# Packed attention and a token-mixing MLP on one core: two heads by 64 partitions, 128-token query tiles, 64x32 PV tiles, single PSUM banks, and one computed issue order

## The chip, the cores and the metric

The kernel runs on one core of one Trainium2 chip. The metric is the device time of one execution in microseconds (us). "The kernel before" took 183.92 us (median of three runs, 183.14 to 187.25). Some executions of one kernel take longer at a lower granted clock; a run over 1.5% above the fastest of its kernel is called slow, and the ratios below use the other, fast runs alone, with a 95% interval.

Engines are named as in the profile: PE is the TensorE matmul, PEld its weight load, DVE the VectorE, ACT the ScalarE, POOL the GpSimd, SP the SyncE. A "q" after a name (SPq) is the engine's instruction queue, for example while it issues a DMA.

## The reference

Eight batches, eight heads, 576 tokens, head width 64, and 32 "pack" queries per head:

```python
def sm_attn(qq, kk, vv):                     # softmax attention, scale 1/8
    s = scale * np.matmul(qq, kk.transpose(0, 1, 3, 2))
    a = softmax(s)
    return np.matmul(a, vv)
p_packed = sm_attn(p, k, v)                  # 32 packed rows per head
x = sm_attn(q, p_packed, p_packed)           # back to 576 tokens
# x as [batch, 576, 512]
W_tok = (x @ w_q) @ (x @ w_k).T / 8          # [576, 576] per batch
out = np.maximum(W_tok @ x, 0) @ w_out       # [batch, 576, 512], float32
```

Neither kernel forms the 576 x 576 matrix: both compute `y` (64 x 512, from `w_k`, the second softmax and the packed rows), then `mix = y^T wq^T`, a relu, and the output product.

## The kernel before

A row of 576 tokens is cut so that each partition holds 18 of them: 32 partitions per head, four heads side by side, two groups of four heads. Three streams run against each other: `stage_a` of batch i+1 (first attention, to the packed rows), `stage_c` of batch i (second attention, to `y`), and `stage_e` of batch i-1 (mix and output). Each is a generator cut into steps, and `together` interleaves the steps in proportion.

```python
    NG, NP = 2, 4
    R, QP = 18, 32
    # PSUM pools: tp (2 banks), sc (2), acc (2 tiles), w (2)
    def rows(x, b):
        return x[b].rearrange("(G pos) (sh sl) d -> (pos sh) G sl d", G=NG, sl=R)

    def load_cast(x, b, name):                       # k and q: cast by the GpSimd's DMA
        t = inpool.tile([P, NG, R, Dh], bf16, tag=name, name=name)
        nc.gpsimd.dma_start(t, rows(x, b))
    def load_v(b):                                   # v: loaded as fp32, cast by POOL
        nc.sync.dma_start(t, rows(v, b))
    # ... first loads, in this order: k0, p0 (POOL's queue), v0 (SP's), q0, weights, p, k1, v1, q1

        def pvm(c):                                  # 144 matmuls per batch, 32x32 tiles
            for r in range(3):
                for par in range(2):
                    s = 2 * (3 * c + r) + par
                    for G in range(NG):
                        for pos in range(NP):
                            m = slice(pos * QP, (pos + 1) * QP)
                            nc.tensor.matmul(
                                pv[m, G, 0:Dh + 1], e1[m, r, G, par, :], v_sb[m, G, s, 0:Dh + 1], ...)

    def stage_e(b, st):
        for j in range(NJ):                          # mix: 64 rows of contraction
            nc.tensor.matmul(ps, y[:, j * P:(j + 1) * P], wqT[:, 0:512], start=True, stop=True)
            nc.scalar.activation(relu[:, j, 0:512], ps, RELU)
            yield
        # ...
        for ci, (c0, sz) in enumerate(chunks):       # five chunks, the last of 64 tokens
            for j in range(NJ):
                nc.tensor.matmul(ps[0:sz], relu[:, j, c0:c0 + sz], wout_w[:, j, :], ...)
                if j == 1:
                    yield
            # ... copy to o
            for i in range(sz // QP):                # 18 output DMAs of 64 KB per batch
                nc.sync.dma_start(o_v[c, x, r], o[i * QP:(i + 1) * QP])
            yield

    def together(*streams):
        todo = []
        for order, (steps, gen) in enumerate(streams):
            todo += [((i + 0.5) / steps, order, gen) for i in range(steps)]
        for _, _, gen in sorted(todo, key=lambda x: x[:2]):
            next(gen, None)
```

The softmax here doesn't subtract the row's maximum and nothing guards it: scores larger than these inputs give would overflow.

## Time and profile before

| | before |
|---|---|
| median of runs | 183.92 us |
| span of the profiled run (its time 187.25 us) | 185.8 us |
| PE busy, whole span | 139.5 us (75%) |
| first score transposes / first query score | 14.5 / 31.0 us |
| one batch in the steady state | 17.6 us |
| last `y` copy to the end | 16.0 us |

The profiled run is the longest of the three. Its clock explains that: see the PEclk row below.

The first fence is from the page of the kernel before: the span, the busy time of each engine (share of the span, number of instructions), the clock granted to PE in 40 slices (tenths of full speed), and the chain of waits that ended last, by engine.

```profile
span 185.8 us, 6608 instructions
...
PE 139.5 (75%) x2854; PEld 89.6 (48%) x2880; DVE 87.2 (47%) x197; ACT 74.8 (40%) x164; POOL 68.4 (37%) x75
...
PEclk9999999975559999999999999999999999999996
...
PE 45%; DVE 18%; DMA 9%; issue 7%; ACT 7%; SPq 5%; POOL 5%; DVEq 0%; POOLq 0%; ACTq 0%
```

The second fence is the windows view of the kernel before. The cuts are at ScalarE's copies of `y`, one per batch. The columns after the window are its length, each engine's busy time and number of instructions, the granted clock, the DMA share and the GB/s.

```profile
core 0: us, PE busy (x) PEld busy (x) DVE busy (x) ACT busy (x) POOL busy (x), PEclk, DMA share, GB/s
45.70:66.60 20.90, 19.51 (x352) 12.72 (x349) 9.73 (x22) 9.00 (x21) 9.05 (x11) 0.74 0.51 101
66.60:154.50 87.90, 79.05 (x1760) 50.23 (x1781) 51.12 (x115) 44.38 (x101) 35.22 (x34) 1.00 0.64 163
154.50:169.80 15.30, 11.71 (x118) 7.04 (x120) 7.86 (x17) 7.36 (x17) 3.14 (x3) 1.00 0.31 79
169.80:185.80 16.00, 6.81 (x30) 2.44 (x28) 3.44 (x5) 3.59 (x7) 0.00 (x0) 0.91 0.38 98
```

The second row holds five batches: 87.90 / 5 = 17.6 us each, PE busy for 79.05 of 87.90 us (90%). The row above it is a batch partly at half clock, and it took 20.9 us.

The third fence is the chain of waits of the kernel before through one steady batch, from one `y` copy to the next (start, duration, what; short pieces left out).

```profile
84.28 0.60 ACT y L336
...
87.54 0.56 DVE qT L242
...
88.56 0.60 DVE rs L257
...
89.65 1.05 POOL a_1955 L261
...
92.16 0.55 PE out_ps L357 x2
...
92.73 0.70 DVE o_sb L365
...
93.45 0.31 SPq L369
...
95.26 1.65 SPq L369
...
97.90 1.64 DMA out_dram<-o_sb
...
99.55 0.70 DVE o_sb L365
...
100.30 0.59 PE out_ps L357 x2
...
101.86 0.60 ACT y L336
```

### The profile page before, as it was taken

How to read it: one execution, taken by the hardware profiler on the slowest of the kernel's cores; microseconds unless marked ns; L12 is line 12 of the kernel's file. 1: busy time of each engine (PE TensorE's matmuls, PEld its weight loads, DVE VectorE, ACT ScalarE, POOL GpSimd, SP SyncE). 2: the span in 40 equal slices, each digit the busy share in tenths (PEclk: the TensorE clock that was granted, in tenths of full speed). 3: DMA queues.
4: the chain of work that ended last, by engine and by line, in shares of the span. 5: the costliest groups of instructions: out<-in, count | busy, mean ns of one | idle time of the engine just before them, and what ended most of it. 6: DMA issues, size and time to landing. Idle time of an engine off the chain costs nothing.

```text
span 185.8 us, 6608 instructions
## 1 busy us (share of the span) xinstructions
PE 139.5 (75%) x2854; PEld 89.6 (48%) x2880; DVE 87.2 (47%) x197; ACT 74.8 (40%) x164; POOL 68.4 (37%) x75
## 2 busy tenths in 40 slices
PE   0008457768999889988998998799979987787820
PEld 0006436654766556645663665376546654443300
DVE  6004024832357348545754673468357633743220
ACT  2002114324453356336633753483347436625400
POOL 7636045335424372445327342704352420420000
PEclk9999999975559999999999999999999999999996
DMA  5999999990941489849964996374450144044153
GB/s 187 335 237 183 256 283 213 280 257 12 179 79 31 120 138 246 299 105 156 282 240 90 207 322 190 93 175 163 109 131 11 40 106 115 4 112 121 49 141 87
DMA packets 17133, 29.66 MB, mean 160 GB/s; under 512 B 5840, under 2 KB 6352, under 8 KB 17104
## 3 DMA queue, kind: packets, MB, share of 16 engines
q0 software_dynamic: 8016, 10.36, 33.4%
q1 hardware_dynamic: 9088, 18.88, 32.9%
q8 instruction: 22, 0.36, 0.8%
q14 instruction: 7, 0.06, 0.1%
HBM read 30.15 MB, written 9.44 MB: 213 GB/s over the span
## 4 chain that ended last, share of the span: by engine, by line
PE 45%; DVE 18%; DMA 9%; issue 7%; ACT 7%; SPq 5%; POOL 5%; DVEq 0%; POOLq 0%; ACTq 0%
PE out_ps L357 11%; DVE o_sb L365 6%; DMA k_sb<-in_k_dram 6%; PE e_ps L248 5%; SPq L369 5%; PE qT_ps L238 5%; PE pv_ps L178 5%; PE kT_ps L152 4%; DMA out_dram<-o_sb 3%; PE mix_ps L344 3%; DVE rs L257 3%; DVE qT L242 3%; PE aT_ps L268 3%; ACT y L336 3%; PE e_ps L165 2%
## 5 line engine op out<-in xcount | busy, mean ns | idle before, releaser
L357 PE MATMUL out_ps<-wout_w,relu 128*128 128x512 bf16 (+1 forms) x134 | 41.1, 382 | 4.4 <-DVE o_sb L365 2.1
L365 DVE COPY o_sb<-out_ps 128x512 f32<-128x512 f32 (+1 forms) x32 | 22.1, 690 | 20.1 <-PE out_ps L357 13.4
L242 DVE COPY qT<-qT_ps 128x768 bf16<-128x768 bf16 x24 | 13.4, 557 | 19.1 <-PE qT_ps L238 19.1
L207 POOL TENSOR_TENSOR ppb<-pp,mask 128x256 bf16<-128x256 bf16 x16 | 10.4, 671 | 32.4 <-DVE pp L202 32.4
L345 ACT ACTIVATE relu<-mix_ps 128x512 bf16<-128x512 f32 x32 | 18.8, 596 | 7.7 <-PE mix_ps L344 7.7
L357 PEld LDWEIGHTS <-relu 128*128 128x128 bf16 (+1 forms) x160 | 12.8, 101 | 10.8 <-issue 8.1
L248 PEld LDWEIGHTS <-qT 128*96 128x96 bf16 x192 | 12.1, 135 | 7.4 <-DVE qT L242 4.8
L152 PE MATMUL kT_ps<-ident,k_sb 128*128 128x128 bf16 x144 | 14.4, 248 | 0.7 <-DVE kT L156 0.7
L156 DVE COPY kT<-kT_ps 128x768 bf16<-128x768 bf16 x24 | 13.3, 552 | 3.3 <-PE kT_ps L152 2.5
L238 PE MATMUL qT_ps<-ident,q_sb 128*128 128x128 bf16 x144 | 13.7, 239 | 1.2 <-ACT pT L127 1.2
L344 PE MATMUL mix_ps<-wqT,y 64*128 64x512 bf16 x32 | 13.2, 412 | 1.2 <-ACT y L336 0.8
L269 DVE COPY aT<-aT_ps 128x384 bf16<-128x384 bf16 x24 | 7.6, 316 | 13.1 <-PE aT_ps L268 13.1
L136 PE MATMUL pT_ps<-ident,p_nat 128*64 128x128 bf16 x32 | 2.1, 312 | 14.1 <-POOL ident masks.py:199 14.1
L238 PEld LDWEIGHTS <-q_sb 128*128 128x128 bf16 x144 | 9.6, 108 | 5.0 <-issue 4.9
L324 ACT ACTIVATE wqT<-wq_ps 64x288 bf16<-64x288 f32 x16 | 6.5, 404 | 13.3 <-PE wq_ps L322 13.3
L152 PEld LDWEIGHTS <-k_sb 128*128 128x128 bf16 x144 | 10.8, 112 | 1.5 <-issue 1.0
L363 ACT ACTIVATE o_sb<-out_ps 128x512 f32<-128x512 f32 x8 | 4.8, 597 | 12.8 <-PE out_ps L357 11.6
L275 PE MATMUL wk_ps<-pqk,aT 128*96 128x64 bf16 x96 | 8.7, 213 | 0.7 <-issue 0.5
L165 PE MATMUL e_ps<-pT,kT 128*32 128x64 bf16 x576 | 9.2, 202 | 0.0
L278 ACT ACTIVATE wk<-wk_ps 96x128 bf16<-96x128 f32 x24 | 6.4, 268 | 5.8 <-PE wk_ps L275 5.7
L136 PEld LDWEIGHTS <-p_nat 128*64 128x64 bf16 x32 | 1.8, 167 | 14.2 <-DMA p_nat<-in_p_dram 12.0
L85 POOL CAST v_bf_86<-v_in 128x2304 bf16<-128x2304 f32 x4 | 8.5, 2116 | 0.0
(292 smaller groups left out, 239.6 us busy)
## 6 DMA issues: line engine op xcount, KB each, us to landing
v_in<-in_v_dram SPq DMA_DIRECT2D x8, 1152.0 KB, 9.9
out_dram<-o_sb SPq DMA_DIRECT2D x144, 64.0 KB, 1.7
k_sb<-in_k_dram POOLq DMA_DIRECT2D x8, 576.0 KB, 8.9
q_sb<-in_q_dram POOLq DMA_DIRECT2D x8, 576.0 KB, 11.4
wout_w<-in_moe_w_out_dram POOLq DMA_DIRECT2D x1, 512.0 KB, 17.2
p_nat<-in_p_dram POOLq DMA_DIRECT2D x1, 224.0 KB, 12.2
wqk<-in_moe_w_q_dram POOLq DMA_DIRECT2D x1, 64.0 KB, 11.7
wqk<-in_moe_w_k_dram POOLq DMA_DIRECT2D x1, 64.0 KB, 11.4
```

The source lines that it names most:

```text
L152: nc.tensor.transpose(ps[:, r, G, :], k_sb[:, G, s:s + 2, :].rearrange("a r d -> a (r d)"), ident)
L156: nc.vector.tensor_copy(kTs[c], ps)
L165: nc.tensor.matmul(ps[m, r, G], kT[:, r, G, m], pT[:, b, G * NP + pos], start=True, stop=True)
L178: nc.tensor.matmul(pv[m, G, 0:Dh + 1], e1[m, r, G, par, :], v_sb[m, G, s, 0:Dh + 1], start=s == 0 and G == 0, stop=s == R - 1, skip_group_ ...
L207: nc.gpsimd.tensor_tensor(ppb[:, G], pp[:, G, 0:1, :].to_broadcast((P, NP, Dh)), mask, op=MULT)
L238: nc.tensor.transpose(ps[:, r, G, :], q_sb[:, G, s:s + 2, :].rearrange("a r d -> a (r d)"), ident)
L242: nc.vector.tensor_copy(qTs[c], ps.rearrange("a r G (pos s) -> a (G pos) r s", s=QP))
L248: nc.tensor.matmul(ps[:, :, h, :], qT[:, h].rearrange("a r s -> a (r s)"), ppT[:, h], start=True, stop=True)
L344: nc.tensor.matmul(ps, y[:, j * P:(j + 1) * P], wqT[:, 0:512], start=True, stop=True)
L345: nc.scalar.activation(relu[:, j, 0:512], ps, RELU)
L357: nc.tensor.matmul(ps[0:sz], relu[:, j, c0:c0 + sz], wout_w[:, j, :], start=j == 0, stop=j == NJ - 1)
L365: nc.vector.tensor_copy(o[0:sz], ps[0:sz])
```

## The change

Its stated intent is another layout and another way of issuing:

- two heads by 64 partitions, nine rows of tokens on each, so a batch fills the partitions with four pairs of heads;
- query tiles of 128 tokens instead of 96; the rests of 64 tokens of two batches share one output tile;
- PV as 72 matmuls on 64x32 tiles into two banks, instead of 144 on 32x32 tiles;
- the mix contracts over 128 rows (half of them zero), and wq and wk come out of one group of matmuls;
- 8 single PSUM banks, named one by one, instead of pools;
- the first k block is loaded first, uncast, in two halves; v is cast by its DMA and no longer by POOL;
- output DMAs of up to 512 KB, 20 in all, instead of 144 of 64 KB;
- all steps of all batches issued from one list, `ORDER`, that was computed beforehand.

The diff, cut to its core:

```diff
+ORDER = """
+LD.v0 LD.q0 LD.W0 LD.W1 PX.0=0 PXb.0 PXa.0 LD.PRA LD.k1 KT.0.0=0 KT.0.1=1 KE.0.0 KE.0.1 LD.v1
+S1.0.0=1 LD.q1 KT.0.2=0 X1.0.0 KT.0.3=2 KE.0.2 KT.0.4=3 KE.0.3 KE.0.4 S1.0.1=2 S1.0.2=3 X1.0.1
 ... (step.batch.part=bank; some 55 lines)
+"""
-    NG, NP = 2, 4
-    R, QP = 18, 32
+    U, R, G = 4, 9, 64
     def rows(x, b):
-        return x[b].rearrange("(G pos) (sh sl) d -> (pos sh) G sl d", G=NG, sl=R)
+        return x[b].rearrange("(u i) (g r) d -> (i g) u (r d)", i=2, r=R)
 ...
+    k0 = rows(k, 0)
+    nc.sync.dma_start(k32[:, 0:2], k0[:, 0:2])
+    nc.sync.dma_start(k32[:, 2:4], k0[:, 2:4])
 ...
+    MCH = ((0, 8), (8, 16), (16, 18))
+    def PV(b, c, bk=None):
+        m0, m1 = MCH[c]
+        for f in range(2 * m0, 2 * m1):
+            u, r = f // R, f % R
+            for i in range(2):
+                rhs = ...                                # 64 columns of v and 64 of ones
+                nc.tensor.matmul(T["pv", b][i][u * L:(u + 1) * L, :],
+                                 T["e1", b][halves(i), f // 2, f % 2, :], rhs,
+                                 start=r == 0, stop=r == R - 1, skip_group_check=True)
 ...
+    def MX(b, j, bk):
+        nc.tensor.matmul(ps, T["y", b][:, j * P:(j + 1) * P], rhs, start=True, stop=True)
 ...
+    def OE(b, t):                                        # two tiles, then one 512 KB DMA
+        copy("AVAV"[t], o[:, t % 2], T["ot", b, t])
+        if done[b, tp] == 2:
+            nc.sync.dma_start(dst.rearrange("g (s m) -> g s m", s=2), ...)
 ...
     with tc.manual_schedule():
-            together(*streams)
+        for item in ORDER.split():
+            name, _, bk = item.partition("=")
+            f = name.split(".")
+            if f[0] == "LD":
+                load(f[1])
+                continue
+            steps[f[0]](*args)
```

In `ORDER`, KT/QT are the key and query transposes, S1/S2 the scores, X1/X2 the exponentials, RS/RR/AM the second softmax (AM on POOL), AT its transpose, WKQ, GM and Y the steps to `y`, MX/RL the mix and relu, OT/OE the output product and copy, LD a load. KE, QE, AE, WE, GE and YE are the copies of these results out of PSUM.

## The prediction

> **What bounds the kernel now.** Three stretches.
> (1) Start: the chain of waits begins with the first k load (issued at 1.2 us, landed 11.8 us), behind 2.3 MB of v; the first score transposes run at 14.5 us, the PE then waits 3.5 us for no visible reason ("issue", 20.9 us, probably instruction fetch), and the first q transposes run only at 29.5 us.
> (2) Steady state: the y copies of ScalarE, one per batch, come at 66.6, 84.3, 101.9, 119.7, 137.1, 154.5 us: 17.6 us per batch. By the windows view PE is busy 90% there, DVE 10.2 us, ACT 8.9, POOL 7 per batch. So PE bounds it. From about 39 to 56 us the granted clock is 0.5 and that batch takes 20.9 us.
> (3) Tail: 16 us from the last y copy to the end. SP issues 144 output DMAs at 0.71 us each (41 in 29.1 us) and is behind at the end.
>
> **PE per batch.** The Trainium skill (TensorE: Matmul & The Clock Gate, "Back-to-back issue gap") gives N/2.4+2.5 ns. The timeline agrees: six transposes of 128 take 0.35 us (58 ns), 20 output matmuls 4.67 us (233 ns). From start-to-start times I sum about 16.0 us per batch before. Estimate after:
> - output matmuls 20 to 18 (the 64-row rests of two batches share a tile): 4.6 to 4.0
> - mix at 128 rows instead of 64: four cost 0.36 each now, 0.22 after: 1.44 to 0.9
> - wk and wq merged: 1.6 to 0.9
> - PV 144 matmuls (10 ns each, four tiles at once) to 72 with N=128, two row tiles at once into two banks: 1.5 to about 1.9, a loss
> - S1 72 of 32 columns to 36 of 64: about equal, 0.9
> - transposes: k same, q 18 to 20, aT 12 to 10 of full width; S2 24 at 128 weight columns: equal or slightly less
> Sum about 14.0 us: 2 us less per batch.
>
> **Other engines per batch, estimated from durations in the trace.** POOL loses the v cast (2.12 us). DVE: 10.2 to about 10.3 (two output copies and g fewer, two relus of about 0.66 more). ACT: 8.9 to about 10.3. DMA: v now cast-loaded, input packets 2304 B instead of 4608; output 20 DMAs of up to 512 KB instead of 144. 4.7 MB per batch at about 350 GB/s is 13.5 us: a second bound near PE.
>
> **Critical path.** Start: k0 is loaded first, uncast and in halves; it should land at 5 to 8 us, and the first q scores run at about 16 us instead of 31: 12 to 14 us gained after the slower fp32 transposes. Steady: 7 x 2 = 14 us. Tail: about 5 us (split relus, SP queue empty). Together 32 us from 184: 152. Counted otherwise: PE saturated from 17 us, 110 us of work at 90%, 6 us of tail: 145.
>
> **Predicted: 148 us, range 139 to 158.** Chances: faster 0.97, within 2% 0.02, slower 0.01.
>
> **What would show it.** y copies 15 to 16 us apart; first q-score matmul before 18 us; PE busy sum near 115 us; 72 PV matmuls in about 1.9 us; no v cast on POOL; SP without lag at the end; last y copy to end 10 to 11 us.
>
> **What would make it wrong.** PV row tiles that don't overlap (then 53 ns each, +2 us per batch, 164 us); 2304-byte packets slow enough that DMA bounds it (PE waiting on k, q, v, 155 to 160); ACT or DVE late in the strict computed order, with PE waiting on bank releases; half clock for long stretches (+3 us each).

## The result, and the profile after

The changed kernel took 137.48 us (median of four runs, 136.22 to 138.82) against 183.72 for the kernel before on the same chip; the ratio of fast runs is 0.749, interval 0.743 to 0.755. Ratios here are the mean time of one kernel's fast runs over that of the other's in the same rounds, so not quite the ratio of the medians quoted. The result is faster than the whole predicted range.

The page of the changed kernel, the same lines:

```profile
span 135.5 us, 4623 instructions
...
PE 114.5 (85%) x1991; PEld 79.8 (59%) x1991; DVE 82.4 (61%) x222; ACT 73.9 (55%) x167; POOL 51.4 (38%) x64
...
PEclk9986998699999999999999999999999999999999
...
PE 66%; ACT 12%; DVE 10%; issue 5%; DMA 2%; ACTq 0%
```

The windows view of the changed kernel; the cut at 30.80 is the first `y` copy, 116.40 and 123.60 the last two, and the second row holds six batches:

```profile
17.00:30.80 13.80, 11.08 (x259) 9.46 (x257) 8.74 (x27) 7.76 (x22) 9.32 (x12) 0.88 1.22 207
30.80:116.40 85.60, 78.14 (x1487) 56.03 (x1485) 57.18 (x142) 52.15 (x119) 30.52 (x35) 1.00 0.84 183
116.40:123.60 7.20, 7.18 (x74) 4.12 (x72) 5.24 (x13) 4.63 (x12) 2.43 (x3) 1.00 0.36 146
123.60:135.50 11.90, 6.45 (x32) 2.41 (x30) 3.18 (x5) 4.37 (x8) 0.00 (x0) 1.00 0.50 199
```

A batch takes 85.60 / 6 = 14.3 us instead of 17.6. PE's busy share in that row is 91%, hardly more than the 90% of before. SPq and the output DMA have nearly left the chain.

Where the 50.3 us between the two profiled spans lie:

| stretch | before | after | difference | predicted |
|---|---|---|---|---|
| start to the first `y` copy | 45.7 | 30.8 | 14.9 | 12 to 14 |
| first to last `y` copy (seven batches) | 124.1 | 92.8 | 31.3 | 14 |
| last `y` copy to the end | 16.0 | 11.9 | 4.1 | 5 |

In the middle stretch PE's busy sum falls from 19.51 + 79.05 + 11.71 = 110.3 to 78.14 + 7.18 = 85.3 us, that is by 25.0, and the rest falls by 6.3 us. The half-clocked batch before was busy 19.51 us against 79.05 / 5 = 15.8 in the five after it, so 3.7 of the 25.0 us are the clock of that run; about 21 us are less busy time in other ways.

PE's busy time per batch in the full-clock windows, worked out from start-to-start times in the two traces (five batches before, six after), beside what the prediction assumed:

| matmuls | before | after | assumed after |
|---|---|---|---|
| output | 4.42 | 3.83 | 4.0 |
| PV | 1.52 | 1.58 | 1.9 |
| mix and its rest | 1.62 | 1.01 | 0.9 (mix alone) |
| k transposes | 1.37 | 1.13 | same as before |
| q transposes | 1.12 | 1.25 | about 10% more |
| second scores | 1.29 | 0.94 | "equal or slightly less" |
| first scores | 0.87 | 0.90 | 0.9 |
| wk and wq | 1.70 | 0.86 | 0.9 |
| aT, g, y and small ones | the rest | the rest | |
| all | 15.8 | 13.0 | 14.0 |
| PE not busy | 1.8 | 1.25 | 1.6 (at 90%) |

In the window of the kernel before, 20 of the 100 output matmuls left no record (there are 100 weight loads and 80 matmuls), so 4.42 is a little low; with the gaps filled in by hand it is about 4.5, an estimate.

So a first theory offers itself. **Theory A:** the mechanism was right (PE bounds the steady state) and only the sum was off: PE's work fell by 2.8 us a batch instead of 2. **Theory B:** PE's work did not set the pace, neither before nor after; the order of the steps did, by keeping PE fed while other engines' links run beside it. Smaller rivals: POOL relieved of the v cast (C), the 128-row mix (D), the earlier start being worth more than its share (E), the merged output DMAs (F).

### The profile page after: what moved, and what is told of

Its sections match the earlier page's. It is cut to its first block, busy times and chain, and to the rows that moved or that the text cites. A ratio compares the mean times of both kernels' runs of the same rounds, so it can differ in the third digit from the quotient of the medians.

```text
span 135.5 us, 4623 instructions
## 1 busy us (share of the span) xinstructions
PE 114.5 (85%) x1991; PEld 79.8 (59%) x1991; DVE 82.4 (61%) x222; ACT 73.9 (55%) x167; POOL 51.4 (38%) x64
## 4 chain that ended last, share of the span: by engine, by line
PE 66%; ACT 12%; DVE 10%; issue 5%; DMA 2%; ACTq 0%
PE out_ps L463 20%; PE pv_ps L274 10%; PE qT_ps L332 6%; PE kT_ps L239 6%; PE aT_ps L381 4%; PE e_ps L256 4%; PE e_ps L350 3%; PE mix_ps L433 3%; ACT relu L437 2%; PE wkq_ps L401 2%; DMA out_dram<-o 2%; DVE kT L123 2%; PE g_ps L413 2%; ACT e L356 2%; PE wkq_ps L397 2%
## 5 line engine op out<-in xcount | busy, mean ns | idle before, releaser
L463 PE MATMUL out_ps<-wout,relu 128*128 128x512 bf16 x128 | 31.0, 379 | 2.1 <-ACT relu L437 1.7
L372 POOL TENSOR_TENSOR a<-e,rr 128x512 bf16<-128x512 f32 (+1 forms) x24 | 21.2, 901 | 29.9 <-DVE rr L367 25.8
L463 PEld LDWEIGHTS <-relu 128*128 128x128 bf16 x128 | 11.6, 98 | 13.9 <-ACT relu L437 2.5
L123 DVE COPY qT<-qT_ps 128x1024 bf16<-128x1024 bf16 (+1 forms) x24 | 13.2, 595 | 6.7 <-PE qT_ps L332 6.6
L274 PE MATMUL pv_ps<-v_sb,e 64*32 64x128 bf16 x576 | 13.7, 221 | 1.3 <-issue 1.3
L362 DVE TENSOR_REDUCE rs<-e 128x16 f32<-128x512 f32 (+1 forms) x24 | 13.3, 576 | 1.3 <-ACT e L356 1.2
L274 PEld LDWEIGHTS <-e 64*32 64x32 bf16 x576 | 11.9, 95 | 2.9 <-issue 2.5
L332 PE MATMUL qT_ps<-idb,q_sb 128*128 128x128 bf16 x160 | 11.3, 219 | 2.5 <-issue 1.7
L356 ACT ACTIVATE e<-e_ps 128x512 f32<-128x512 f32 (+1 forms) x24 | 11.5, 535 | 3.4 <-PE e_ps L350 3.1
L262 ACT ACTIVATE e<-e_ps 128x512 bf16<-128x512 f32 (+1 forms) x24 | 10.8, 491 | 4.0 <-PE e_ps L256 3.9
L437 ACT ACTIVATE relu<-mix_ps 128x512 bf16<-128x512 f32 x16 | 10.9, 755 | 0.3 <-PE mix_ps L433 0.2
L123 DVE COPY kT<-kT_ps 128x1024 bf16<-128x1024 bf16 (+1 forms) x21 | 10.5, 545 | 0.4 <-PE kT_ps L239 0.4
```

Source lines behind the costliest of these rows:

```text
L123: nc.vector.tensor_copy(o, i)
L262: nc.scalar.activation(e1[:, m0:m1], T["s1", b, c], EXP, scale=scale)
L274: nc.tensor.matmul(T["pv", b][i][u * L:(u + 1) * L, :], T["e1", b][halves(i), f // 2, f % 2, :], rhs, start=r == 0, stop=r == R - 1, skip_ ...
L332: nc.tensor.transpose(ps[:, n, u, :], q_in[b][:, u, o:o + P], idb)
L356: nc.scalar.activation(e2, T["s2", b, c].rearrange("a t i u l -> a (t i u) l"), EXP, scale=scale)
L362: nc.vector.tensor_reduce(rs, T["e2", (b, c)], axis=AX, op=ADD)
```

## The experiments

All kernels gave correct results. Kernels of one call ran on one chip with their own runs of the kernel before, and the ratio is against those. Medians are of all runs, ratios of fast ones.

| label | median us | ratio of fast runs |
|---|---|---|
| e9_after_again (the changed kernel once more) | 137.82 | 0.753 [0.745, 0.761] |
| e1_pv_serial | 140.54 | 0.760 [0.750, 0.770] |
| e8_pv_rounds | 138.39 | 0.750 [0.733, 0.768] |
| e2_mix64 | 139.32 | 0.754 [0.745, 0.763] |
| e7_before_mix128 | 183.26 | 0.995 [0.978, 1.012] |
| e3_plain_order | 163.01 (fast run 159.35) | none, one fast run |
| e10_plain_later_aT | 154.19 | 0.835 [0.815, 0.855] |
| e4_k0_late | 139.61 | 0.756 [0.746, 0.765] |
| e13_no_warm | 138.56 | 0.752 [0.747, 0.757] |
| e5_pool_cast | 138.89 | 0.758 [0.750, 0.765] |
| e6_out_split | 157.44 | 0.847 [0.838, 0.857] |
| e11_start_tail | 133.34 | 0.722 [0.717, 0.728] |
| e16_start_tail_again | 133.60 | 0.727 [0.717, 0.737] |
| e12_start_tail_pv | 134.24 | 0.729 [0.725, 0.734] |
| e14_new_order | 138.72 | 0.755 [0.748, 0.763] |
| e15_new_order_pv | 141.27 | 0.769 [0.759, 0.779] |
| e17_new_order2 | 127.54 | 0.697 [0.693, 0.702] |
| e18_new_order2_pv | 129.73 | 0.711 [0.706, 0.715] |

### The control

e9_after_again is the changed kernel without an edit.

> The changed kernel itself (one blank line more), as the standard for the other runs on this chip. 136 to 139 us, ratio to before 0.74 to 0.755.

Measured 137.82 us, 0.753. Differences of about one per cent between calls are noise.

### Is it PE's work? More of it, and less of it

e1_pv_serial issues all PV matmuls of one row half before those of the other, so that neighbours in the list share a tile:

```diff
-        for f in range(2 * m0, 2 * m1):
-            u, r = f // R, f % R
-            for i in range(2):
+        for i in range(2):
+            for f in range(2 * m0, 2 * m1):
+                u, r = f // R, f % R
```

> Edit: in PV all matmuls of one row half (one tile, one bank) are issued before those of the other half, so that neighbouring matmuls can no longer overlap as two row tiles. Same work, same order of steps. Theory 'the PE's own work sets the pace, and the PV pairs overlap': 72 PV matmuls go from 1.5 us to 3.5 to 3.9 us (53 ns each), the whole from 137.5 to 150 to 156 us. Rival 'the pace is set by the computed order and by evictions, the PE has slack': under 142 us. If pairs did not overlap in the changed kernel, nothing moves at all.

Measured: the PV stage, from its first start to its last, went from about 1.4 to 2.09 us per batch (from 1.58 to 2.32 as the table above counts), less than expected. Matmuls of one tile start 56 ns apart in this trace; in this order 60 of the 72 follow one in the same tile, which would give 60 x 56 ns = 3.4 us if none could start ahead of an earlier one. The start times show a second stream woven in (gaps of 6 and 50 ns, then 16 and 40), which suggests that matmuls of different tiles that are not neighbours in the list ran beside each other; the records do not say which matmul is which. The total rose by 1.5 us (by the ratios) to 3 us (by the medians) where 8 x 0.7 = 5.6 us of PE work were added: at most about half of it showed.

e8_pv_rounds does the reverse. It holds PV back until all exponentials are there and walks the eight tiles in rounds:

```diff
-        for f in range(2 * m0, 2 * m1):
-            u, r = f // R, f % R
+        if c < 2:
+            return
+        for f in range(2 * 18):
+            u, r = f % U, f // U
+            f = u * R + r
```

> Edit: the 72 PV matmuls are issued together, in nine rounds over all eight tiles (four column groups by two row halves), after the last exp. The sums are the same. Theory 'a tile takes one N=128 matmul per 53 to 56 ns, and tiles run side by side': 0.55 to 0.9 us of PE time instead of 1.4 to 1.5 us, so 0.6 us per batch; as far as PE sets the pace the whole falls by 3 to 5 us against the changed kernel. Rival 'the PE has slack in the computed order': under 1 us, or longer, because PV now starts later.

Measured: PV per batch fell from 1.58 to 0.85 us, as intended. The windows views of the control e9 and of e8, each from its first to its seventh `y` copy:

```profile
30.61:116.66 86.05, 79.16 (x1479) 56.92 (x1486) 57.43 (x142) 52.55 (x119) 30.48 (x35) 0.98 0.84 183
```

```profile
32.26:117.60 85.34, 74.42 (x1479) 52.87 (x1486) 57.63 (x142) 52.41 (x119) 30.53 (x35) 0.98 0.82 181
```

PE's busy time fell from 79.2 to 74.4 us, and the time in which it stood idle rose from 6.9 to 10.9 us. The ratio is 0.750 against 0.753 of the control on the same chip: no gain is seen, though the interval (0.733 to 0.768) still allows one of 2%. The edit also starts PV later, and no run separates that from the smaller amount of work. It speaks against A, but less than it seems, for this reason:

**A pause that no releaser explains.** These are the longest waits of PE between those `y` copies, first in the changed kernel, then in e8_pv_rounds. The profile finds nothing that PE waited for ("issue"):

```profile
PE qT_ps L332 <- issue: 1.7, 1, 1.7
...
PE g_ps L413 <- issue: 1.4, 1, 1.4
PE pv_ps L274 <- issue: 1.3, 1, 1.3
```

```profile
PE qT_ps L334 <- issue: 2.2, 1, 2.2
PE g_ps L415 <- issue: 2.0, 1, 2.0
PE pv_ps L276 <- issue: 1.7, 1, 1.7
```

In the changed kernel these pauses stand 512 PE records (weight loads and matmuls) apart. In all kept traces together there are 47 such pauses of over 0.4 us after the first 8 us, and each ends 1.2 to 1.6 us after a 16 KB transfer of the DMA queue that the page calls "instruction" has ended. So PE had very probably run ahead of its own instructions; no run varied this. The pauses take 4.4 us of the changed kernel (of 7.5 us in which PE is idle in that stretch), 3.7 in e9, 5.9 in e8, 1.5 in e1, and there are none in e3 and e10 below. Of e8's 4.0 us of new idle time, 2.2 are longer pauses; e1 lost 2.2 to 2.9 us of them. After the change PE's work and these pauses together fill 82.5 of 85.6 us, so e1 and e8 do not show that PE had time to spare.

e7_before_mix128 takes one reduction of PE's work back into the kernel before: its mix contracts over 128 rows, half of them zero.

```diff
+    y_bufs = [const.tile([P, D], bf16, name=f"y{i}") for i in range(2)]
+    wqT_bufs = [const.tile([P, S], bf16, name=f"wqT{i}") for i in range(2)]
+    for t in y_bufs + wqT_bufs:
+        nc.gpsimd.memset(t, 0.0)
 ...
-            nc.scalar.activation(wqT[:, half * hs:(half + 1) * hs], wps, COPY, scale=scale2)
+            nc.scalar.activation(wqT[0:Dl, half * hs:(half + 1) * hs], wps, COPY, scale=scale2)
 ...
-        nc.scalar.activation(y, yps.rearrange("a G n -> a (G n)"), COPY)
+        nc.scalar.activation(y[0:Dl], yps.rearrange("a G n -> a (G n)"), COPY)
```

> Edit of the kernel before: the mix matmuls read 128 rows, of which 64 are zeros, as in the changed kernel. Prediction's reading 'PE bounds the kernel before': 0.3 to 0.6 us less PE time per batch, the whole -2.5 to -5 us (179 to 181.5). Rival 'its batches are bound by chains between the engines': within 1.5 us of 184.

Measured 0.995, interval 0.978 to 1.012; the ratio alone cannot exclude the 1 or 2% that were at stake, so the windows decide. The windows view of e7_before_mix128 over the same five batches:

```profile
61.10:148.80 87.70, 77.35 (x1781) 49.58 (x1781) 50.68 (x115) 44.28 (x100) 35.27 (x34) 1.00 0.64 164
```

PE was busy 77.35 us instead of 79.05, and five batches took 87.70 us instead of 87.90. What PE was spared, 1.7 us, became idle time, 1.5 of it. One batch spoils this comparison: it took 18.51 us and holds 1.06 us of the pauses described above (one batch of the kernel before, 17.80 us long, holds 0.46). The other four took 17.31 us each, and in the kernel before 17.70, 17.58, 17.41 and 17.41: 0.1 to 0.4 us came through per batch, 0.2 on average, of some 0.4 that PE was spared. Where the rest went can be seen: PE's wait before `aT` grew from 0.35 to 0.66 us in every batch. The runs' times agree: 181.84 and 182.11 us at a mean clock of 0.99, against 181.87 to 183.53 for the five runs of the kernel before with a clock of 0.98 or more, so not the 2.5 to 5 us less that were expected. So PE's work alone did not set the pace of the kernel before in its steady state, at 90% busy; about half of what it was spared showed. This is the finding against the first sentence of the prediction's steady stretch. It also shows the start, middle and tail without the half clock (this run had none before its last 3.3 us): 44.0, 120.0 and 16.0 us, so that of the 31.3 us of the middle 27.2 remain.

e2_mix64 gives the changed kernel its 64-row mix back:

```diff
-        nc.tensor.matmul(ps, T["y", b][:, j * P:(j + 1) * P], rhs, start=True, stop=True)
+        nc.tensor.matmul(ps, T["y", b][0:Dl, j * P:(j + 1) * P], rhs[0:Dl], start=True, stop=True)
```

> Edit: the mix matmuls read 64 rows instead of 128 (the lower 64 are zeros, the result is the same), as in the kernel before. Theory 'a 64-row tile between 128-row ones costs a change of tile mode': the four mix matmuls and four rest ones go from about 1.0 us to 1.5 to 1.7 us of PE time per batch, the whole +3 to +5 us (140.5 to 142.5). Rival 'the mix was dear before only because other streams were cut in between': within 1 us of 137.5.

Measured: mix and rest cost 0.24 us more per batch, less than expected, and the total moved by 1 to 2 us at most (0.754). Theory D is out as a main source: the eight matmuls on 64 rows are not dear. The prediction put the step from 1.44 to 0.9 us down to the 128 rows; about half of it comes from them (0.24 us here, 1.62 - 1.33 = 0.29 in e7).

### Is it the order?

e3_plain_order keeps every instruction of the changed kernel (same layout, loads, DMAs and start) and replaces the list from the second batch on by what the kernel before does: three streams, cut into the same steps, interleaved in proportion, banks handed out to whatever came free first.

```diff
 ORDER = """
 ... (first batch as in the changed kernel)
-PXb.3 S2.0.2=5 PXa.5 PXb.4 PXa.6 X2.0.0 PXa.7 RS.0.1 X2.0.2 PXb.6 RS.0.0 PXb.7 LD.v3 KT.1.0=3
-RR.0.1 KT.1.2=7 RR.0.0 KT.1.1=5 KE.1.0 AM.0.0 KE.1.1 S1.1.0=3 AM.0.1 KE.1.2 S1.1.1=5 RS.0.2
+PXb.3 S2.0.2=5 PXa.5 PXb.4 PXa.6 X2.0.0 PXa.7 RS.0.1 X2.0.2 PXb.6 RS.0.0 PXb.7 LD.q3 LD.v3
+KT.1.0=4 KE.1.0 KT.1.1=1 KE.1.1 RR.0.0 AM.0.0 S1.1.0=6 X1.1.0 KT.1.2=2 KE.1.2 RR.0.1 AM.0.1
 ...
```

> Edit: the steps of the changed kernel in the plain proportional interleaving of the kernel before (output stage of batch i-1, key stage of i+1, query stage of i), PSUM banks given out least recently used; the start up to the first score sums is kept. Theory 'the layout's smaller PE work carries the gain': 141 to 149 us, PE busy sum about 114 us as in the changed kernel, more idle time. Rival 'the computed order carries what the prediction missed': 150 us or more, at or above the 148 that was predicted from work alone.

Measured: one fast run at 159.35 us, three slow ones up to 163.64. Even the fast one gives back 22 of the 46 us. The profile of e3_plain_order is of a slow run, so only its waits and its steady stretch, at a clock of 0.98, are used. The windows view over five of its batches, and the longest waits of PE (who waited for whom: us in total, times, longest):

```profile
52.20:137.70 85.50, 72.57 (x1226) 47.00 (x1227) 48.08 (x115) 44.66 (x98) 24.44 (x27) 0.98 0.58 133
```

```profile
PE aT_ps L382 <- POOL a L373: 11.6, 8, 1.7
PE mix_ps L434 <- ACT y L428: 3.5, 7, 0.7
```

A batch takes 85.50 / 5 = 17.1 us: the new layout in the old manner of issuing runs at nearly the old pace of 17.6. PE arrives at the transpose of the second softmax before POOL is through with it, eight times, for 11.6 us.

e10_plain_later_aT is the same plain order with those transposes and what hangs on them one or two steps later (shown are the steps of one turn, parted by bars, from which the list was made; they are not lines of the kernel):

```diff
-  RS1 RR1 AM1 AT0 AE0 | S22 X22 | WKQ0 WE0 | RS2 RR2 AM2 AT1 AE1 | WKQ1 WE1 | AT2 AE2 | WKQ2 WE2 | ...
+  RS1 RR1 AM1 | S22 X22 | AT0 AE0 RS2 RR2 AM2 | WKQ0 WE0 | AT1 AE1 | WKQ1 WE1 |  | AT2 AE2 | WKQ2 WE2 | ...
```

> Edit against the plain order of the earlier run: the transposes of a batch's normalised scores are put one to two steps later, so that other work of PE stands between GpSimd's product and its reader. Theory 'the plain order loses its time where PE waits for GpSimd's product (11.6 us in 8 waits there)': 147 to 155 us, PE's wait for that product under 3 us. Rival 'any plain proportional order is bound by the length of the three chains in a turn': 158 us or more.

Measured 154.19 us, 0.835. Its windows view over five batches (a fast run) and its longest waits of PE:

```profile
49.70:129.70 80.00, 70.38 (x1215) 46.42 (x1227) 47.94 (x115) 44.53 (x99) 24.36 (x27) 1.00 0.66 155
```

```profile
PE e_ps L350 <- DVE qT L123: 5.6, 8, 0.8
PE mix_ps L433 <- ACT y L427: 3.7, 8, 0.7
...
PE aT_ps L381 <- POOL a L372: 1.6, 3, 0.9
```

The wait for POOL shrank from 11.6 to 1.6 us, a batch to 16.0 us, and the next links, DVE's copy of the query transposes and ACT's copy of `y`, came forward. These two runs are the strongest evidence for B: with the layout and every instruction held fixed, the order (with its bank numbers) alone is worth about 15 us (e10, by the ratios of fast runs) to 22 us (e3's only fast run), more than the 10.5 us by which the prediction was off. It is also seen that "busy" is not work: the same list of matmuls is busy 122.8 us in e10's whole span and 114.5 in the changed kernel's, which had more half clock (6.8 us against 3.4). In the trace an output matmul takes 216 ns when the next one follows at once, and 244 ns on average in e7's five batches of the old layout (all 100 recorded), whose steps issue them in pairs.

### The start and the tail

e4_k0_late lets the first k block come through POOL's casting queue, behind v0:

```diff
-LD.v0 LD.q0 LD.W0
+LD.v0 LD.k0 LD.q0 LD.W0
-    nc.sync.dma_start(k32[:, 0:2], k0[:, 0:2])
-    nc.sync.dma_start(k32[:, 2:4], k0[:, 2:4])
```

> Edit: the first k is loaded as all others (cast to bf16 by the software queue, behind the first v), not first, uncast and in halves. Theory 'the early k0 is worth its head start': k0 lands at 10 to 12 us instead of 5.3 and 7.6, the first k transposes start at 10 to 12 us instead of 7.4, the whole +3 to +5 us (140.5 to 142.5). Rival 'the start is bound by q0 and k1, which come later on the same queue': under +1.5 us, or more than +5 if q0 and k1 slip by the 3 us of one more load and everything behind them with it.

Measured: k0 landed at 10.29 us, the first transposes ran at 10.33 (7.43 in the changed kernel) and the first query score at 20.76 (17.80). Three microseconds of later start cost about 2 in the total by the medians, 0.5 to 1.3 by the ratios. E is out: the start is worth its share and no more.

e13_no_warm drops the nine warm-up matmuls (`WARM = 9` to `WARM = 0`).

> Edit of the changed kernel: no warm-up matmuls. Theory 'they only keep the granted clock up in the start': half clock in the first 10 us, k transposes and scores of batch 0 slower, +0.5 to +2 us. If they do nothing: within 0.7 us of 137.8.

Measured 138.56 us, 0.752: at most 1 us, within noise.

e11_start_tail takes out three small waits seen in the trace: the clearing of a 7-batch buffer before the first copies of k, two banks shared in the first batch, and the last output DMA that waits for two tiles.

```diff
-    zero(pdiag[:, 1:].rearrange("a b x h l -> a (b x h l)"))
+        if b == 0 and c == 0:
+            zero(pdiag[:, 1:].rearrange("a b x h l -> a (b x h l)"))
-KT.0.0=0
+KT.0.0=4
-QT.0.1=0
+QT.0.1=6
+        if b == B - 1:
+            nc.sync.dma_start(dst.rearrange("g (s e n) -> g s e n", s=2, e=2)[:, :, t % 2], o[:, t % 2])
+            return
```

> A version meant to beat both. Three edits of the changed kernel: the 1.55 us clearing of the later batches' p buffer moves from before the first p copy into an idle stretch of VectorE; the first k transposes and the first q transposes get PSUM banks that nobody holds; the last batch's output goes out in four DMAs of 256 KB, not two of 512. First k transposes at 5.5 us instead of 7.4, first PV at 10 to 11 instead of 13, last DMA shorter by 0.7 us. If the start is worth its full time: 134 to 135.5 us, ratio 0.73 to 0.74. If, as with the late k0, about 0.6 of a shift at the start reaches the end: 135 to 136.5. Rival 'the start is bound by the loads behind it': no change but the tail, 137.

Measured 133.34 us, 0.722. The first query score ran at 14.58 us, the first `y` copy at 27.9 instead of 30.8, and every later one some 3 us earlier too, the last at 120.6 instead of 123.6; the last stretch is 0.8 us shorter. A start 3 us earlier passed through in full.

e12_start_tail_pv is e11 with e8's PV, and e16_start_tail_again repeats e11.

> The same with PV in nine rounds over eight tiles. If PE work counts again once the start is earlier: 1 to 4 us below the version without it. If PE has slack in this order, as the run of PV rounds alone said: within 1 us of it.

> The changed kernel with the earlier start and the split last output again, as the standard on this chip: 132.5 to 134.5 us.

Measured 134.24 us for e12, on e11's chip: again no gain from 0.7 us less PV per batch, rather a loss of 1 us. Its profiled run had 13.7 us at half clock, e11's 3.4, and 5.8 us of PE's pauses without a releaser, e11's 4.2. The repeat gave 133.60.

### POOL and the output DMAs

e5_pool_cast puts a cost like the old v cast back on POOL, as two copies of dead data in each batch's `PB` step:

```diff
     def PB(b):
+        for _ in range(2):
+            nc.gpsimd.tensor_copy(junk_o, junk_i)
```

> Edit: GpSimd gets back the load of the old v cast, two copies of 128x1152 fp32 to bf16 per batch (about 2.1 us), just before the masked product. Rival theory 'taking the cast off GpSimd made the query chain (reciprocal, GpSimd product, aT) shorter and carries the unforeseen gain': +8 us or more. Theory 'PE work and order': GpSimd is at 38%, +0 to +3 us, only where the copies stand before a product that PE waits for.

Measured 138.89 us, 0.758: about 1 us more than the control on the same chip. C is out as a main cause.

e6_out_split issues each 512 KB output DMA as eight of 64 KB, as before:

```diff
-            nc.sync.dma_start(dst.rearrange("g (s m) -> g s m", s=2),
-                              o.rearrange("a e n -> a (e n)"))
+            for z in range(8):
+                nc.sync.dma_start(dv[z * 8:(z + 1) * 8], ov[z * 16:(z + 1) * 16])
```

> Edit of the changed kernel: each output DMA of 512 KB is issued as eight of 64 KB, so that SP again issues about 130. Theory 'few output DMAs shorten the tail, because SP issues one in 0.4 to 0.7 us': steady state unmoved, the last one or two batches' DMAs queue, +2 to +4 us (139.5 to 141.5). Rival 'the tail is shorter only through the relus and the order': under +1 us.

Measured 157.44 us, 0.847: 18 us (fast runs) to 20 us (medians) more, far above the expectation. The timeline of e6_out_split, first the last work of PE, then the last output DMAs of SP (start, duration, what):

```profile
126.10 3.63 PE L463 MATMUL out_ps<-wout,relu 128*128 128x512 bf16 x16 [0.19 <-ACT relu L437]
```

```profile
117.71 22.76 SPq L481 DMA_DIRECT2D out_dram<-o  x32
140.57 0.38 SPq L470 DMA_DIRECT2D out_dram<-o_rem  x1
141.06 11.32 SPq L481 DMA_DIRECT2D out_dram<-o  x16
```

PE is finished at 129.7 us, as in the changed kernel, and its busy sum is the same; SP is still issuing at 152.4, at 22.76 / 32 = 0.71 us for each DMA. The 128 issues alone are some 91 us of SP's queue (128 x 0.71), and their tiles are ready only in the last three quarters of the run. So F holds as a condition, not as the source of the speed: at this pace the old output DMAs would have cost most of what the order gives. In the kernel before, the same queue is 6.1 us of a batch's chain.

### A better order

The order in the changed kernel was given. If B is right, another order of the same work should move the time, without any change to PE's work. e14_new_order is e11 with the list after the first batch recomputed: a small scheduler played the program forward with the durations measured in the trace of the changed kernel, took at each point a ready step by the length of the chain behind it, and varied those priorities at random for the shortest end.

> The same program (earlier start, split last output, PV as in the changed kernel), only the order of the steps and their PSUM banks computed anew, by a list scheduler that uses the durations measured in the traces of this case. Theory 'the order turns the work into time and the given one still leaves idle PE time': 123 to 129 us. Rival 'the given order is near what these dependencies allow': 131 us or more.

Measured 138.72 us, slower than e11 (133.60 on that chip). The longest wait of PE in e14_new_order:

```profile
PE aT_ps L382 <- POOL a L373: 9.4, 3, 8.6
```

POOL stood at load instructions at that time. No load from the ninth on was issued before the load eight before it had landed (issued at 18.62, 21.22, 24.68 and 27.01 us, after landings at 18.09, 20.94, 24.15 and 26.73), and POOL's arithmetic queues behind them. The trace shows where this comes from: the program's loads on this queue use eight completion semaphores in turn, and these loads wait for the one that the load eight before them raises. The scheduler did not know it and had placed loads early. e15_new_order_pv, the same with e8's PV, met it too, with a wait of 8.6 us for a v block:

> As the run of the new order, with PV in rounds over eight tiles (0.7 us less PE work per batch) and the order computed for it. Theory 'PE work counts once the order is made for it': 3 to 6 us below the new order alone. Rival 'another limit (chains through VectorE, ScalarE and GpSimd, or loads) is reached': within 1.5 us of it.

It took 141.27 us.

e17_new_order2 is e14 with this rule in the scheduler: no load before the eighth before it has landed. The code is that of e11, only the list differs:

```diff
-PXb.3 S2.0.2=5 PXa.5 PXb.4 PXa.6 X2.0.0 PXa.7 RS.0.1 X2.0.2 PXb.6 RS.0.0 PXb.7 LD.v3 KT.1.0=3
-RR.0.1 KT.1.2=7 RR.0.0 KT.1.1=5 KE.1.0 AM.0.0 KE.1.1 S1.1.0=3 AM.0.1 KE.1.2 S1.1.1=5 RS.0.2
+PXb.3 S2.0.2=5 PXa.5 PXb.4 PXa.6 X2.0.0 PXa.7 RS.0.1 X2.0.2 PXb.6 RS.0.0 PXb.7 KT.1.2=1
+KT.1.0=6 KT.1.1=2 LD.v3 KE.1.2 KE.1.0 S1.1.2=1 X1.1.2 KE.1.1 S1.1.0=6 RR.0.1 X1.1.0 S1.1.1=2
 ...
```

> New order as before, loads held back until the eighth before them has landed. No stall of GpSimd at a load; PE's longest wait under 2 us. Theory 'the order turns work into time': 124 to 131 us, below the 133.5 of the same program in the given order. Rival 'the given order is near what the dependencies allow': 132 us or more without such a stall.

Measured 127.54 us (126.54 to 128.04), 0.697. The page of e17_new_order2, and its windows view from 30.0 us, 2 us before the first `y` copy, to the last one:

```profile
span 124.8 us, 4605 instructions
...
PE 110.2 (88%) x1978; PEld 78.6 (63%) x1991; DVE 82.6 (66%) x222; ACT 74.1 (59%) x167; POOL 51.2 (41%) x64
...
PE 77%; DMA 12%; DVE 3%; issue 2%; POOL 1%; ACT 1%; ACTq 0%
```

```profile
30.00:105.30 75.30, 73.50 (x1468) 54.99 (x1478) 56.44 (x140) 50.87 (x117) 33.53 (x39) 1.00 0.92 193
```

PE is now busy 73.50 of 75.30 us (98%) and 77% of the chain, and those of its pauses without a releaser that are over 0.4 us take 0.7 us in all. (In this order the `y` copies come 5.8 to 21.3 us apart and no longer mark batches; 19.5 us follow the last one.) The same program as e11 in another order is 6 us faster by the medians, 5 by the ratios, and it beats both kernels: 30% less than the kernel before.

e18_new_order2_pv is the same with e8's PV and an order computed for it.

> The same with PV in rounds (0.7 us less PE work per batch) and the order computed for it. Theory 'PE work counts once the order is made for it': 2.5 to 6 us below the run beside it. Rival 'another limit is reached': within 1.5 us.

Measured 129.73 us, 2.2 us slower than e17 although PE has some 0.7 us less to do per batch. Its profiled run had 10.2 us at half clock, and its runs were granted 0.94 to 0.953 on average; e17's had 0.963 to 0.994. It also had 5.4 us of PE's pauses without a releaser, e17's 0.7. Whether less PE work pays once PE is 98% busy therefore stays open: the lighter version never ran at the same clock, nor without these pauses.

## Why the prediction was right or wrong

**Right: the direction and the start.** The first query score was predicted at about 16 us instead of 31 and ran at 17.8; 12 to 14 us were predicted for the start, and the profile shows 13.2 by that score, 14.9 by the first `y` copy. e4 and e11 show that such microseconds pass through, in e4 only in part.

**Right: the tail.** 5 us predicted, 4.1 measured; 10 to 11 us from the last `y` copy to the end predicted, 11.9 measured.

**Right in number, not in meaning: PE's busy sum.** "Near 115 us" was predicted and 114.5 measured. But of this, 11.6 us lie before 17 us (114.5 less the 102.9 in the windows from there on, warm-up and fp32 transposes among it), where the prediction's second count had put 110 us of work after that point.

**Wrong: the step "Steady: 7 x 2 = 14 us".** The middle gave 31.3 us, of which 27.2 remain when the half clock of that profiled run is taken out with the help of e7's. Its seven intervals are not alike: six gave 3.2 us each (104.8 us in e7, 85.6 after), and the last one 8.0 (15.2 to 7.2), where the list leaves PE 7.2 us of work instead of 11.7. Two things failed in the step.

1. *The size.* PE's time per batch fell by 2.8 us instead of 2. PV cost 1.58 instead of 1.9 us. The second scores, the k transposes, aT and g, which were taken as about equal, fell by 1.29 - 0.94, 1.37 - 1.13, 0.70 - 0.60 and 0.52 - 0.36 = 0.85 us in all. Taken at its face, seven batches of 0.8 us are 5.6 us of the miss.
2. *The mechanism.* The step took "PE is busy 90%, so PE bounds it" and turned PE microseconds into time. It gave the order of the steps no part. e7 took some 0.4 us per batch from PE, and about half of it came through. e8, e12 and e18 took 0.7 us per batch from it after the change, and nothing was gained, but their pauses without a releaser grew by 2.2, 1.6 and 4.7 us, and e12 and e18 ran at a lower clock; e1 added as much, and half of it showed. Part of what looked like PE work was PE spread out by its order (e10: busy 122.8 us for the matmuls that are busy 114.5 in the changed kernel). So Theory A falls as the whole explanation. Of Theory B it is shown that the order decides how well PE is filled; that PE's work does not count after the change is not shown.

**What stood in its place: the order.** With everything else of the change in place, the old manner of interleaving gives 159 us (e3's fast run), with one chain moved back 152 to 154 (e10's fast runs), the given list 137.5 to 137.8, and a list computed from measured durations 127.5 (on e11's start and tail, which alone give 133.4). The layout in plain order lies close to the 152 us of the prediction's first count. The prediction saw the computed order only as a risk ("ACT or DVE late in the strict computed order") and credited it with nothing. It is worth 15 us or more. e10 puts a number on the failed step: in that plain order the middle takes 106.4 us, 13.6 less than the 120.0 of e7 and close to the 14 foreseen; the given list takes off another 13.6 (92.8). In e3's plain order the middle takes 114.4 us, in a slow run. The second count, "110 us of work at 90%" from 17 us on, fell to the same two faults: from 17 us PE was busy 102.9 of 118.5 us.

**Enabled by: the merged output DMAs.** With 64 KB DMAs the changed kernel takes 157 us, because SP cannot issue them fast enough at 0.71 us each (e6). The prediction named SP's lag only for the tail.

**The clue was in the profile.** In the chain of waits of the kernel before, PE had 45%, and a steady batch's chain passed through DVE, POOL, SPq and an output DMA. The Trainium skill, Perfetto Trace Analysis, section "Identifying the Most-Contended Engine", says that matmul busy share is not a good measure of how close a kernel is to the hardware's limit, and points to the weight-load share among others. This agrees: over the middle windows shown above the matmul busy share went from 90 to 91% although a batch became 3.3 us shorter, while PEld went from 57 to 65%, and to 73% in e17. The prediction used the chain of waits for the start alone.

**The risks that were named.** PV's row tiles do overlap: 72 matmuls take about 1.4 us, where one after the other at 56 ns would take 4.0. The smaller input packets did not make DMA the bound: PE's longest wait with a releaser between the first and the seventh `y` copy is 1.5 us for ACT's relu, and none that the view lists there is for a load. The half clock came and went: 17 us of it in the profiled run before, 6.8 after.

**What stays open.** Why stretches of half clock come; why PE's instructions come late at some points, and what an earlier supply would give; whether less PE work pays at 127 us; how much the merged output DMAs alone would give the kernel before, which was read from its chain and not tried; and what a computed order would give with the old layout. Only three orders on e11's program and three on the changed kernel's were run, so the 127.5 us are no limit.

## What to carry to other kernels

An engine that is 90% busy need not be the bound: remove a little of its work and see whether the time follows, and read the share of each engine in the chain of waits first. Then look for pauses without a releaser: they can swallow what an experiment adds or takes away, as they did here. Where several batches overlap on engines that issue in order, the interleaving can be worth more than a tile layout; compute it from measured durations, and put the queue limits of the loads into the model. Merging output DMAs may show no gain in bytes and still be what lets the rest of the schedule run.

## What the Trainium skill lacked or had wrong

- TensorE: Matmul & The Clock Gate. (1) Its section "The mechanism", in the part on packing small matmuls, states that matmuls start and end strictly in program order. In e1_pv_serial the 72 PV matmuls, 60 of them behind one of the same tile, took 2.09 us, where that order with the 56 ns seen between two of the same tile gives 3.4 us. The records do not say which matmul of the list each one is, so either the order is not strict or neighbours in a tile can be closer than 56 ns. (2) Its section "Back-to-back issue gap" gives 81 ns for 128 columns and 131 ns for 512 in a real stream of weight loads and matmuls, and 56 and 216 ns for the isolated gap; the transposes here, each with its own weight load, stayed at 56 ns, and the output matmuls at 216 ns for 512 columns, which agrees with the isolated formula. (3) Its section "What's actually happening" ties the half clock to an idle window of about 3.4 us. The kernel before had some 17 us of half clock between 39.5 and 56.5 us while PE was busy most of the time (15.49 of these 17.0 us, and 2.63 of the 3.4 us before them). Two of the profiled runs with a lighter PV (e12, e18) had 13.7 and 10.2 us of it where their counterparts (e11, e17) had 3.4 and none, but the third (e8) had 10.2, as had the control e9.
- TensorEngine Tiling (Array Packing), section "Key Properties": it says that a change of tiling mode drains the engine, without a figure. e2_mix64 shows 0.24 us per batch for eight matmuls on 64 rows between 128-row ones.
- DMA: Bandwidth & Descriptors, section "Issuing engines are not separate DMA queues": it calls the time to initiate a DMA usually small beside the DMA itself. Here SP spent 0.71 us on each 64 KB DMA, and splitting 16 DMAs into 128 cost 18 to 20 us (e6_out_split).
- No page that was read says that the built program lets a load on the GpSimd queue wait until the eighth before it has landed, with POOL's arithmetic behind it: 9.4 us of waits for PE in e14_new_order. By the trace it is a limit of the built program (eight semaphores in turn), not one shown of the chip.
